# Four loads for K's first weights, a mix moved behind two squares, and one transposing read in two parts

## The chip, the cores and the metric

The kernel runs on one core of one Trainium2 chip. The metric is the device time of one execution in microseconds (us). Before the change the median of four runs is 413.9 us (413.32 to 414.71).

## What is computed

The input `x` holds 8 sequences of 4160 tokens with 192 channels. Cut to what matters, with all tensors in float32:

```python
y = sum over k of softmax(weight)[h, k] * x[b, s + k - 6, h, g]   # 7 taps, causal, 8 heads of 24 channels
y_prev = y shifted by one token (zeros in front)
xk = y_prev + mu_k * (y - y_prev)
xr = y_prev + mu_r * (y - y_prev)
k  = relu(xk @ w_k) ** 2        # 192 -> 1024
r  = sigmoid(xr @ w_r)          # 192 -> 192
out = r * (k @ w_v)             # 1024 -> 192
```

## The kernel before

**Tiling.** The 8 sequences are handled as 4 pairs; the two sequences of a pair lie on the two halves of the 128 partitions (64 channels of one third of the 192 on each half, three thirds). The tokens of a pair are cut into *steps*. For the first pair these are tokens 0 to 255 (step 0), 256 to 767 (step 1), and so on by 512: step 2 from 768, step 3 from 1280, the fifth step (step 4) from 1792 to 2303, step 5 from 2304 to 2815. A step of 512 tokens has 8 *slots*; each makes one `ps_k` tile of 128 hidden columns by 2 x 512 tokens (`k_mm`, line 537; 12 matmuls of 256 tokens in step 0, 6 of 512 elsewhere). ScalarE turns it into `k_sb` with a ReLU (`k_relu`, line 549), VectorE squares it into `k2` (`k_square`, line 563). Four slots make a *bundle*; bundles are the beat of the program. Slots 0 and 1 are of step 0 and use columns 0 to 255 and 256 to 511 of `w_k`; slots 2 to 5 are of step 1 and use columns 0 to 511; slots 6 and 7 are of step 0 again and use columns 512 to 1023. Step 4's eight slots are bundles 7 and 8, so the seventh bundle (b = 6) is the last one ahead of it.

**Mixing.** For each step VectorE makes `d` (`diff`, line 480), then multiplies it by `mu` for each third (`scale`, line 511, three instructions), then adds `y_prev` over all three thirds (`add_y`, line 517). This is done for `xk`, which `k_mm` reads, and for `xr`, which `r` reads (line 594). `r_out` (line 605) is the sigmoid on ScalarE. `v_rows` (line 625) multiplies `k2` by `w_v`, and `v_out` (line 641) multiplies the result by `r` into `o_sb` on VectorE and sends it out on SyncE's queue (line 649).

**Convolution.** It is done on TensorE in *groups* of blocks. Groups 0 to 2 write `y` already transposed (`conv_t`, line 371, copied by `to_yT`, line 381). Group 3 is turned by TensorE. From the fifth group (group 4) on, `y` goes through DRAM: ScalarE copies it out of PSUM (line 319), `y_write` sends it with four DMAs to `y_dram` (line 424), and `y_read` fetches it back with one transposing DMA into `yT` (line 432). Group 4 holds tokens 1920 to 3039 of the first pair, 1120 rows; its four writes hold, in order, its rows 0-279, 560-839, 280-559 and 840-1119. Step 4's `diff` is the first that needs these rows.

**Order.** The order on each engine is written by hand: tables (`mix_a`, `mix_b`, `mix_c`, `late`, ...) say what runs at which place of which bundle. In `bundle_rest` VectorE gets, in this order: the square of the last bundle's fourth slot, `mix_a`, `v_out`, [here TensorE gets the bundle's first two slots], `mix_b`, the squares of the first two slots, `mix_c`, the square of the third. PSUM is a ring of four tiles shared by all that TensorE makes; a new tile waits until the tile four back has been read. `k_sb` has four buffers.

**Prologue.** `x` for group 0 comes over the two hardware queues. GpSimd (POOL) issues all other loads, which also cast float32 to bf16: `x` of group 1 (line 136), the first half of `w_k` in two loads, one for each half of the partitions (line 208), `x` of group 2, the second half of `w_k`, `x` of group 3, `w_r` (line 197), `w_v` (line 221), `x` of group 4. POOL's DMAs use eight semaphores in turn, so the ninth and each later one waits until the one eight before it has landed.

Of the kernel before, what the change touches and what calls it, by code (L numbers as in the profile page):

```python
# [14 lines left out]
def kernel(  # L15
# [11 lines left out]
    nc = tc.nc  # L27
# [4 lines left out]
    DF = moe_w_k.shape[1]  # L32
# [7 lines left out]
    HB = 56  # L40
# [5 lines left out]
    YC = 16  # L46
# [56 lines left out]
    def x_tile(g):  # L103
        p, base, nb, _, on_pe = groups[g]
        xb = three.tile([P, GB, 2, D], BF16, tag="xb", name="xb")
        xbs[g] = xb
        if g > 4:

            nc.vector.memset(xb[0:1, 0, 0, 0:2], 0.0)  # L109
        if base == 0:  # L110
            nc.gpsimd.memset(xb[0:32, 0, :, :], 0.0)  # L111
        if not on_pe and base + 2 * nb * HB > S:
            n0 = nb - (base + 2 * nb * HB - S) // HB - 1
            nc.gpsimd.memset(xb[Q:P, n0:nb, :, :], 0.0)

    def load_x(g):
        p, base, nb, _, on_pe = groups[g]
        xb = xbs[g]
        if on_pe:
            parts, step, rows = ((0, base),), BLK, P  # L120
        else:
            parts, step, rows = ((0, base), (Q, base + nb * HB)), HB, Q
        for s in range(2):
            b = 2 * p + s
            for q0, start in parts:
                lo, hi = 0, nb
                t0 = start - HALO
                if t0 < 0:
                    lo = 1
                    nc.gpsimd.dma_start(out=xb[HALO:rows, 0, s, :], in_=x[b, 0 : rows - HALO, :])  # L130
                while t0 + (hi - 1) * step + HALO + step > S:
                    hi -= 1
                    r0 = t0 + hi * step
                    if r0 + HALO < S:
                        nc.gpsimd.dma_start(out=xb[q0 : q0 + S - r0, hi, s, :], in_=x[b, r0:S, :])
                nc.gpsimd.dma_start(  # L136
                    out=xb[q0 : q0 + rows, lo:hi, s, :],
                    in_=bass.AP(
                        tensor=x.tensor,
                        offset=x.offset + (b * S + t0 + lo * step) * D,  # L140
                        ap=[[D, rows], [step * D, hi - lo], [1, D]],
                    ),
                )

    def load_x_first(eng, q0, q1, n0, n1, s0, s1):

        rows = [[D, q1 - q0]]
        rest = [[BLK * D, n1 - n0]] if n1 - n0 > 1 else [[S * D, s1 - s0]]
        eng.dma_start(
            out=x_f32[q0:q1, n0:n1, s0, :] if n1 - n0 > 1 else x_f32[q0:q1, n0, s0:s1, :],  # L150
            in_=bass.AP(
                tensor=x.tensor,
                offset=x.offset + (s0 * S + n0 * BLK - HALO + q0) * D,
                ap=rows + rest + [[1, D]],
            ),
        )

    def load_mu(i, m):
        nc.sync.dma_start(
            out=mu_raw[i * NC : (i + 1) * NC, :].rearrange("c (s q) -> c s q", s=2),  # L160
            in_=bass.AP(tensor=m.tensor, offset=m.offset, ap=[[Q, NC], [0, 2], [1, Q]]),
        )
# [43 lines left out]
    def load_wk(c0, c1):  # L206
        for st in range(2):
            nc.gpsimd.dma_start(
                out=wk[st * Q : (st + 1) * Q, :, c0:c1],
                in_=bass.AP(  # L210
                    tensor=moe_w_k.tensor,
                    offset=moe_w_k.offset + c0,
                    ap=[[DF, Q], [Q * DF, NC], [1, c1 - c0]],
                ),
            )

    def load_wr():
        load_thirds(wr, moe_w_r, D)
# [22 lines left out]
    def masks_tap():  # L241

        nc.gpsimd.affine_select(
            out=tap8.rearrange("p (c r) -> p c r", r=8),
            in_=ones_t[0:8, 0:8].unsqueeze(1).to_broadcast([8, P // 8 + 1, 8]),
            pattern=[[0, P // 8 + 1], [-1, 8]],
            compare_op=ALU.is_equal,
            fill=0.0,
            base=0,
            channel_multiplier=1,  # L250
        )

    def select_equal(t, n):
        nc.gpsimd.affine_select(
            out=t,
            in_=(ones_t if t is ident else ones6)[0:n, 0:n],
            pattern=[[1, n]],
            compare_op=ALU.is_equal,
            fill=0.0,
            base=0,  # L260
            channel_multiplier=-1,
        )
# [4 lines left out]
    def masks_band():  # L267
        nc.gpsimd.affine_select(
            out=band, in_=ones_t, pattern=[[-1, P]], compare_op=ALU.is_ge, fill=0.0, base=0, channel_multiplier=1
        )  # L270
        nc.gpsimd.affine_select(
            out=band, in_=band, pattern=[[1, P]], compare_op=ALU.is_ge, fill=0.0, base=K - 1, channel_multiplier=-1
        )
# [11 lines left out]
    ys, yTs, y_drams = {}, {}, {}  # L285
# [143 lines left out]
    def y_read(g):  # L429
        p, base, nb, _, _ = groups[g]  # L430
        r0, r1 = base, min(base + 2 * nb * HB, S)
        nc.sync.dma_start_transpose(
            out=yTs[p][:, :, YC + r0 : YC + r1], in_=y_drams[p][r0:r1, :]
        )


    def tr(g, j):
# [239 lines left out]
    early, rq, rs, xt, mix_a, mix_b, mix_c, vq, late = ({} for _ in range(9))  # L677

    def at(table, b, fn, *a):
        table.setdefault(b, []).append((fn, a))  # L680
# [7 lines left out]
    for g, (p, base, nb, fb, on_pe) in enumerate(groups):  # L688
# [12 lines left out]
        if g > 4:  # L701

            b = {5: 1, 6: 3, 7: 7}.get(g)
            b = first_bundle[first_step[p]] + (-15, -11, -7, -3)[(g - 6) % 4] if b is None else b
# [3 lines left out]
    for s, (p, t0, L, n0, ns) in enumerate(steps):  # L708
        fb = first_bundle[s]
        if s == 0:  # L710
            at(mix_a, 1, mix, s, 1)
            continue
        if s == 1:
            at(mix_b, 1, scale, s, 1, 0, 1)
            at(late, 2, scale, s, 1, 2)
            at(late, 2, add_y, s, 1)
        else:
            if s == 2:
                at(mix_c, 1, diff, s)
            elif s == 4:  # L720
                at(mix_b, fb - 1, diff, s)
            else:
                at(mix_c, fb - 2, diff, s)
            at(mix_b if s == 4 else mix_a, fb - 1, scale, s, 0, 0)
            at(mix_b, fb - 1, scale, s, 0, 1, 2)
            at(mix_c, fb - 1, add_y, s, 0)
            if s == 2:
                at(mix_a, fb, scale, s, 1, 0)
                at(mix_b, fb, scale, s, 1, 1)
            else:  # L730
                at(mix_c, fb - 1, scale, s, 1, 0)
                at(mix_a, fb, scale, s, 1, 1)
            at(mix_b, fb, scale, s, 1, 2)
            at(mix_b, fb, add_y, s, 1)
        if s == LAST - 1 or s < LAST and steps[s + 1][0] > p:
            at(late, fb - 1, keep_tail, p)
    for s, j, vb in quads:
        b = vb - (s == LAST)
        if 0 < s < LAST - 1:
            b = min(b, first_bundle[s + 2] - 2 + j)  # L740
# [11 lines left out]
    def warm(ps, n):  # L752
        for i in range(n):
            nc.tensor.matmul(out=ps[:, i % 2, :], lhsT=ones_t, rhs=zeros, start=True, stop=True)

    def prologue():
        nc.sync.dma_start(
            out=w_raw,
            in_=weight,
        )  # L760
        nc.vector.memset(x_f32[0:32, 0, :, :], 0.0)
        nc.vector.memset(ones_t, 1.0)
        for st, eng in ((0, nc.scalar), (1, nc.sync)):
            load_x_first(eng, 0, P, 1, groups[0][2], st, st + 1)
        load_x_first(nc.scalar, 16, P, 0, 1, 0, 2)
        load_x_first(nc.sync, HALO, 16, 0, 1, 0, 2)
        load_mu(0, moe_mu_k)
        load_mu(1, moe_mu_r)
        nc.scalar.preload_act_table(AF.Exp)
        nc.vector.memset(zeros, 0.0)  # L770
        nc.vector.memset(w_nrm, 0.0)
        nc.vector.memset(ones6, 1.0)
        x_tile(1)
        load_x(1)
        masks_tap()
        select_equal(ident6, 2 * NC)
        masks_band()
        load_wk(0, DF // 2)

        for i in range(SHORT):  # L780
            q = slice(i % 4 * 32, i % 4 * 32 + 32)
            nc.tensor.matmul(
                out=warm_ps[q, 0, 0:1], lhsT=ones_t[:, 0:32], rhs=ones_t[:, 0:1], start=True, stop=True
            )
        warm(warm_ps, WARM[0])
        x_tile(2)
        softmax()
        warm(warm_ps, WARM[1])
        make_toe()
        load_x(2)  # L790
        load_wk(DF // 2, DF)
        select_equal(ident, P)
        x_tile(3)
        load_x(3)
        load_wr()
        load_wv()
        x_tile(4)
        load_x(4)
# [194 lines left out]
```

## Time and profile before

| what | value |
|---|---|
| median of four runs | 413.9 us |
| profiled execution | 413.77 us |
| its span | 412.1 us (1.67 us lie around it) |
| PE busy | 403.2 us, 98% |
| DVE busy | 370.5 us, 90% |
| ACT busy | 353.3 us, 86% |
| POOL busy | 64.3 us, 16% |
| granted TensorE clock | 1.0 |

PE is TensorE, PEld its weight loads, DVE VectorE, ACT ScalarE, SP SyncE (SPq its queue of DMA issues). A timeline line gives the start in us, the duration in us, engine, line, operation, output <- input with shapes, and the count of merged instructions; in brackets stands how long the engine was idle before it and what released it. Merged instructions overlap a little at their ends, so the next one can start before the duration is over. The chain is the sequence of work and waits that ended last, in order of time. A waits view lists who waited for whom.

### The profile page before, as it was taken

Reading aid. Unit: us, or ns where it says so; the run is one execution under the profiler, and the core shown is the slowest. Engines: PE = TensorE matmul, PEld = TensorE weight load, DVE = VectorE, ACT = ScalarE, POOL = GpSimd, SP = SyncE. Lnnn points to the kernel's source line nnn. Section 1 sums busy time; section 2 is a strip of 40 time slices with the busy share of each in tenths; the row PEclk is TensorE's granted clock in tenths of the full one; section 3 lists DMA queues with packets and bytes.
Section 4 is the critical chain, followed back from the end, with each engine's and each line's share of the span. In section 5 each row is a group of like instructions: output and inputs, shape, how many; then the busy total and the mean of one; then the engine's idle time right before and its main releaser. Section 6 shows DMA issues by size and latency. Waiting matters only on the chain.

```text
span 412.1 us, 16799 instructions
## 1 busy us (share of the span) xinstructions
PE 403.2 (98%) x7349; PEld 302.1 (73%) x7350; DVE 370.5 (90%) x672; ACT 353.3 (86%) x426; POOL 64.3 (16%) x100
## 2 busy tenths in 40 slices
PE   7899999999999999999999999999999999999996
PEld 5667767777877776777777777677777777777795
DVE  5899899999999998999999999999989898999973
ACT  6899988889888888989888899888889888887781
POOL 8623023022040202104040110304000000000000
PEclk9999999999999999999999999999999999999999
DMA  9999989989979895998859697896863917321223
GB/s 142 193 202 191 196 196 199 248 131 193 197 110 234 132 219 112 211 192 130 215 104 231 150 197 182 113 232 123 188 160 104 215 46 182 101 70 49 80 80 115
DMA packets 137241, 65.58 MB, mean 159 GB/s; under 512 B 87356, under 2 KB 137168, under 8 KB 137168
## 3 DMA queue, kind: packets, MB, share of 16 engines
q1 hardware_dynamic: 95840, 48.42, 45.8%
q0 software_dynamic: 40528, 15.53, 33.1%
q8 instruction: 57, 0.93, 0.9%
q10 hardware_dynamic: 800, 0.57, 0.4%
q14 instruction: 16, 0.13, 0.1%
HBM read 31.62 MB, written 37.09 MB: 167 GB/s over the span
## 4 chain that ended last, share of the span: by engine, by line
PE 88%; DMA 4%; DVE 3%; ACT 2%; issue 1%; POOL 1%; SPq 0%; POOLq 0%; DVEq 0%; ACTq 0%
PE ps_v L625 39%; PE ps_k L537 37%; PE ps_r L594 7%; PE ps_c L302 3%; DMA wk<-in_moe_w_k_dram 2%; DMA yT<-y_dram 2%; DVE k L563 1%; PE ps_v L577 1%; ACT k_sb L549 1%; DMA y_dram<-y 1%; ACT y L319 0%; DVE d L480 0%; DVE xr L511 0%; POOL xb L136 0%; SPq L424 0%
## 5 line engine op out<-in xcount | busy, mean ns | idle before, releaser
L549 ACT ACTIVATE k_sb<-ps_k 128x1024 bf16<-128x1024 f32 x260 | 253.1, 1036 | 36.0 <-PE ps_k L537 35.1
L563 DVE TENSOR_TENSOR k<-k_sb 128x1024 bf16<-128x1024 bf16 x260 | 173.0, 687 | 28.7 <-ACT k_sb L549 28.3
L537 PE MATMUL ps_k<-xk,wk 64*128 64x512 bf16 (+1 forms) x1632 | 190.9, 367 | 1.4 <-DMA wk<-in_moe_w_k_dram 1.1
L625 PE MATMUL ps_v<-wv,k 64*128 64x192 bf16 x4032 | 188.2, 243 | 0.2 <-DVE k L563 0.2
L625 PEld LDWEIGHTS <-k 64*128 64x128 bf16 x4032 | 167.8, 94 | 13.6 <-issue 4.1
L537 PEld LDWEIGHTS <-wk 64*128 64x128 bf16 x1632 | 80.8, 94 | 58.7 <-DMA wk<-in_moe_w_k_dram 1.3
L136 POOL DMA_DIRECT2D xb<-in_x_dram x62 | 45.2, 739 | 169.0 <-issue 82.2
L641 DVE TENSOR_TENSOR o_sb<-ps_v,r_sb 128x768 f32<-128x768 f32 x64 | 61.0, 953 | 2.6 <-issue 2.4
L605 ACT ACTIVATE r_sb<-ps_r 128x768 bf16<-128x768 f32 x65 | 53.3, 821 | 10.6 <-PE ps_v L625 9.9
L319 ACT CAST y<-ps_c 128x960 bf16<-128x960 f32 (+5 forms) x84 | 50.7, 684 | 0.0
L594 PEld LDWEIGHTS <-xr 64*128 64x128 bf16 x780 | 34.5, 94 | 14.9 <-issue 0.7
L594 PE MATMUL ps_r<-wr,xr 64*128 64x192 bf16 x780 | 43.1, 243 | 0.2 <-DVE o_sb L641 0.2
L511 DVE TENSOR_SCALAR xr<-d,mu 128x512 bf16<-128x512 bf16 (+1 forms) x102 | 35.4, 351 | 0.0
L480 DVE TENSOR_TENSOR d<-yT 128x1536 bf16<-128x1536 bf16 (+4 forms) x36 | 31.4, 871 | 1.4 <-ACT yT L381 1.0
L511 DVE TENSOR_SCALAR xk<-d,mu 128x512 bf16<-128x512 bf16 (+1 forms) x99 | 32.1, 354 | 0.1
L517 DVE TENSOR_TENSOR xr<-xr,yT 128x1536 bf16<-128x1536 bf16 (+1 forms) x33 | 31.0, 938 | 1.1
L517 DVE TENSOR_TENSOR xk<-xk,yT 128x1536 bf16<-128x1536 bf16 (+3 forms) x33 | 30.5, 924 | 0.1
L302 PEld LDWEIGHTS <-toe 64*64 64x64 bf16 x448 | 9.6, 106 | 11.7 <-issue 10.3
L302 PE MATMUL ps_c<-xb,toe 64*64 64x240 bf16 (+1 forms) x448 | 16.6, 265 | 0.2 <-ACT k_sb L549 0.2
L464 POOL COPY y_tail<-yT 128x195 bf16<-128x195 bf16 x4 | 3.2, 794 | 64.9 <-DMA yT<-y_dram 64.8
L111 POOL MEMSET xb<- 32x384 bf16 x3 | 1.2, 408 | 46.4 <-DVE xb L109 39.2
L371 PEld LDWEIGHTS <-xb 128*32 128x32 bf16 (+3 forms) x264 | 4.9, 112 | 2.4 <-ACT xb L230 1.1
(57 smaller groups left out, 62.8 us busy)
## 6 DMA issues: line engine op xcount, KB each, us to landing
out_dram<-o_sb SPq DMA_DIRECT2D x128, 192.0 KB
xb<-in_x_dram POOLq DMA_DIRECT2D x40, 240.0 KB, 7.9
y_dram<-y SPq DMA_DIRECT2D x44, 210.0 KB
y_dram<-y SPq DMA_DIRECT2D x12, 168.0 KB
xb<-in_x_dram POOLq DMA_DIRECT2D x10, 192.0 KB, 5.9
xb<-in_x_dram POOLq DMA_DIRECT2D x6, 216.0 KB, 4.9
xb<-in_x_dram POOLq DMA_DIRECT2D x6, 144.0 KB, 6.0
wk<-in_moe_w_k_dram POOLq DMA_DIRECT2D x4, 192.0 KB, 7.2
```

What stands on the lines that cost most here:

```text
L136: nc.gpsimd.dma_start(out=xb[q0 : q0 + rows, lo:hi, s, :], in_=bass.AP(tensor=x.tensor, offset=x.offset + (b * S + t0 + lo * step) * D, ap ...
L302: nc.tensor.matmul(out=banks[j * Q : (j + 1) * Q, i, :, :, k * G : (k + 1) * G], lhsT=toe[q, h, q], rhs=xbs[g][q, j * m : (j + 1) * m, :, ...
L319: nc.scalar.copy(out=bass.AP(tensor=y.tensor, offset=y.offset + d, ap=[y.ap[0], [m * 2 * D, 2], [2 * D, m], [Q, 2], [1, b - a]],), in_=bas ...
L511: nc.vector.tensor_scalar(out=t[:, c, :L], in0=diffs[s][:, c, :L], scalar1=mu[:, i, c : c + 1], scalar2=None, op0=ALU.mult)
L517: nc.vector.tensor_tensor(out=o, in0=o, in1=y_of(s, sl, 0), op=ALU.add)
L537: nc.tensor.matmul(out=ps[:, i, f * L : (f + 1) * L], lhsT=wk[r, c, fs], rhs=xk[r, c, :L], start=c == 0 and f == 0, stop=c == NC - 1 and f ...
L549: nc.scalar.activation(out=k_sb, in_=ps.rearrange("p a b -> p (a b)"), func=AF.Relu)
L563: nc.vector.tensor_tensor(out=o, in0=i, in1=i, op=ALU.mult)
L594: nc.tensor.matmul(out=ps[:, i, k * D : (k + 1) * D], lhsT=xr[q, c, ts], rhs=wr[q, c, :], start=c == 0, stop=c == NC - 1,)
L605: nc.scalar.activation(out=r_sbs[s, j], in_=r_ps.pop((s, j))[:, :, 0 : 2 * D], func=AF.Sigmoid)
L625: nc.tensor.matmul(out=v_ps[s, j][:, bank, k * D : (k + 1) * D], lhsT=k2s[s][q, f, t * P : (t + 1) * P], rhs=wv[q, f, :], start=half == 0 ...
L641: nc.vector.tensor_tensor(out=o_sb.rearrange("p (b t) d -> p b (t d)", b=2), in0=v_ps.pop((s, j)), in1=r_sbs.pop((s, j)), op=ALU.mult,)
```

## The change

Three edits. (1) The first half of `w_k` is loaded in two quarters: columns 0 to 255 and then 256 to 511, each with one load for each half of the partitions, four loads of 256 columns instead of two of 512. (2) In bundle 6, step 4's `diff` and its scales for `xk` go from `mix_b` to `mix_c`: from ahead of the squares of the bundle's first two slots to behind them. The add, which was in `mix_c`, stays behind them. (3) Group 4's transposing read is issued as two reads on the same queue: rows 0-447 (tokens 1920 to 2367) and rows 448-1119. The first waits for the first and the third write of group 4, the second for the others.

```diff
-        nc.sync.dma_start_transpose(
-            out=yTs[p][:, :, YC + r0 : YC + r1], in_=y_drams[p][r0:r1, :]
-        )
+        for a, b in ((r0, r0 + 8 * HB), (r0 + 8 * HB, r1)) if g == 4 else ((r0, r1),):
+            nc.sync.dma_start_transpose(out=yTs[p][:, :, YC + a : YC + b], in_=y_drams[p][a:b, :])
...
             elif s == 4:
-                at(mix_b, fb - 1, diff, s)
+                at(mix_c, fb - 1, diff, s)
             else:
                 at(mix_c, fb - 2, diff, s)
-            at(mix_b if s == 4 else mix_a, fb - 1, scale, s, 0, 0)
-            at(mix_b, fb - 1, scale, s, 0, 1, 2)
+            at(mix_c if s == 4 else mix_a, fb - 1, scale, s, 0, 0)
+            at(mix_c if s == 4 else mix_b, fb - 1, scale, s, 0, 1, 2)
             at(mix_c, fb - 1, add_y, s, 0)
...
-        load_wk(0, DF // 2)
+        load_wk(0, DF // 4)
+        load_wk(DF // 4, DF // 2)
```

VectorE's instructions of bundles 6 and 7 up to the first `o_sb` of bundle 7, in the order in which the engine gets them:

```
before: square(b5, 4th) | o_sb | diff, scale x3 | square, square (b6) | add xk | scale xr | square, square | scale xr | o_sb
after:  square(b5, 4th) | o_sb | square, square (b6) | diff, scale x3 | add xk | scale xr | square, square | scale xr | o_sb
```

The POOL queue keeps its order; two issues are added, so the second half of `w_k`, which waited for no semaphore before, now waits for the loads of `x` of group 1, and `x` of group 3 waits for the first two quarter loads.

## The prediction

> **What bounds the kernel now.** I read the page's busy times first, then the chain in order of time, then the timelines of PE, ACT and DVE at the two places that the change touches.
>
> ```profile
> span 412.1 us, 16799 instructions
> PE 403.2 (98%) x7349; PEld 302.1 (73%) x7350; DVE 370.5 (90%) x672; ACT 353.3 (86%) x426; POOL 64.3 (16%) x100
> ```
>
> PE is idle for 412.1 - 403.2 = 8.9 us in all, most of it before 11.6 us. Behind 17 us a bundle without convolution takes PE 5.72 us and one with it 6.37 us, again and again, to the end. So a time that PE loses or wins anywhere stays lost or won, and no edit can win more than PE's idle time near it.
>
> The first place, PE's timeline with two lines of DVE's and one of ACT's:
>
> ```profile
> 10.24 0.28 PE L537 MATMUL ps_k<-xk,wk 64*128 64x256 bf16 x1
> 11.64 4.07 PE L537 MATMUL ps_k<-xk,wk 64*128 64x256 bf16 x47 [1.12 <-DMA wk<-in_moe_w_k_dram]
> 17.24 0.83 PE L537 MATMUL ps_k<-xk,wk 64*128 64x256 bf16 x12 [0.31 <-ACT k_sb L549]
> ...
> 10.94 0.70 DVE L480 TENSOR_TENSOR d<-yT 128x1024 bf16<-128x1024 bf16 x1
> 12.33 0.69 DVE L517 TENSOR_TENSOR xk<-xk,yT 128x1024 bf16<-128x1024 bf16 x1
> ...
> 14.32 1.03 ACT L549 ACTIVATE k_sb<-ps_k 128x1024 bf16<-128x1024 f32 x1
> ```
>
> One matmul of slot 0 runs at 10.24, on the half of `wk` that has landed; the other 47 (slots 0 to 5) wait until 11.64 for the other half of the partitions. DVE finishes the last two thirds of step 1's `xk` at 13.02. ACT's third ReLU, slot 2's, starts at 14.32.
>
> The second place, the chain around bundle 6:
>
> ```profile
> 42.66 6.64 DMA yT<-y_dram
> 49.33 0.97 DVE d L480
> 50.33 0.88 DVE xk L511 x3
> 51.20 1.20 DVE k L563 x2
> 52.41 0.87 DVE xk L517
> ...
> 55.01 0.88 DVE o_sb L641
> 55.89 0.04 issue
> 55.93 0.67 PE ps_r L594 x12
> ```
>
> And the lines of PE, ACT and DVE that go with it:
>
> ```profile
> 53.67 2.11 PE L537 MATMUL ps_k<-xk,wk 64*128 64x512 bf16 x18
> 55.93 0.67 PE L594 MATMUL ps_r<-wr,xr 64*128 64x192 bf16 x12 [0.15 <-DVE o_sb L641]
> ...
> 49.77 1.07 ACT L549 ACTIVATE k_sb<-ps_k 128x1024 bf16<-128x1024 f32 x1
> ...
> 48.15 0.96 DVE L641 TENSOR_TENSOR o_sb<-ps_v,r_sb 128x768 f32<-128x768 f32 x1 [0.21 <-PE ps_v L625]
> 49.33 0.96 DVE L480 TENSOR_TENSOR d<-yT 128x1536 bf16<-128x1536 bf16 x1 [0.22 <-DMA yT<-y_dram]
> ```
>
> The reader is to see how short the wait for the transposing read is: DVE's `o_sb` holds the engine until 49.1, the read lands at 49.30, the wait is 0.22 us. From there DVE runs without a gap to `o_sb` at 55.9, for which PE waits. And bundle 7's first matmul at 53.67 finds `xk` only 0.39 us old (52.41 + 0.87 = 53.28).
>
> **Edit 2, the mix behind two squares.** No instruction is added; what counts is when the two squares may start. They wait for ACT: bundle 6's first ReLU runs 48.85 to 49.92, the second 49.77 to 50.84 (49.77 + 1.07), and ACT has no gap ahead of them (three `y` copies from 47.11 on). So, with the gap of 0.02 that such releases show, and DVE's spacing of 0.61 between a square and what follows:
>
> - first square 49.94, second 50.86 (DVE idle for 0.8 and then 0.3 us)
> - `diff` 50.86 + 0.62 = 51.48; the scales one diff-to-scale step (50.33 - 49.33 = 1.00) later, 52.48
> - the add waits for the third scale: 52.48 + 0.88 + 0.02 = 53.38, done at 54.25 by its chain length (before: 53.28)
> - then scale 0.26, two squares 1.21, scale 0.26, `o_sb` 0.88: done at 56.86 to 56.94 (before 55.89)
>
> Two waits on PE follow. Bundle 7's slots start at about 54.35 instead of 53.67, and `ps_r`, whose PSUM tile `o_sb` must free, at 56.95 instead of 55.93. The second contains the first: **+1.0 us**, and nothing behind it gives that back, since PE has no slack later. The bounds: +0.3 (only the `xk` wait, 0.7, less the about 0.35 that bundle 7 loses already, 55.93 against 55.61 at the pace of the bundles) and +1.3 (another 0.3 if the squares behind slip too).
>
> **Edit 3, the read in two.** DVE will ask for these rows at 51.5 and the whole read landed at 49.30, so an earlier first part is worth nothing with edit 2; without edit 2 it would be worth at most the 0.22 us. Costs: SP is held 3.33 us by the one read; the shortest of the 14 reads holds it 2.59. Two reads hold it 3.33 (by rows) to 5.2 us (twice the shortest). Behind them on SP stand the `out_dram` writes of 46.10; their `o_sb` tile is wanted again three tiles on, at 60.60, and group 5's `y` writes, which ACT releases at 49.0. Both have cover. The second part is wanted by step 5's `diff`, 58.27 before; even at twice 6.64 us from 42.66 it is there at 55.9. **0**, with 0 to +0.2 for a surprise.
>
> **Edit 1, the quarters.** Slot 0 needs only the first quarter, slot 1 the second. In the trace the first half's 384 packets of 1024 B pass at some 110 per us from 6.2 on, and the last of them lands at 11.59; packets of 384 B (`x`) pass at 460 per us. Per engine of the 16 that is 145 and 35 ns. A 512 B packet does not occur; its ends are 47 ns (35 x 512 / 384, by the `x` row) and 145 ns, if a packet costs the same at any length. I take 50 to 70 (half of 145 is 72), nearest to the `x` row in length: 384 of them need 1.2 to 1.7 us, both quarters together no more than the half did. Then the first quarter is there at 10.24 and the second by about 11.6.
>
> The Trainium skill, "DMA: Bandwidth & Descriptors", section "Anatomy of one DMA — SWDGE (gpsimd) path", speaks against this: about 2.0 us of each such DMA are fixed, and only the rest goes by bytes. By its fit a half load of 197 KB would be an estimated 2.45 us and a quarter 2.23, so the first quarter would come 0.2 us earlier and not 1.4, and edit 1 would win next to nothing; the sum would be +0.9. The trace has the half loads landing 5.6 and 6.7 us after their issue behind other traffic, so neither price can be read off directly.
>
> What does PE win? Slot 0 at 10.24 instead of 11.64, slot 1 by 12.3. But slot 2 needs step 1's `xk`, done at 13.02, and before it read the second third at about 13.07. So PE wins nothing there: **the wait for weights becomes a wait for DVE**, whose chain starts at 10.94 and reads no weights. What is won is ACT's: two ReLUs (0.92 each) are out of the way, and the third starts at slot 2's end, about 13.75, instead of 14.32. The fifth ReLU, for which PE waited at 17.24 (0.31 us, a PSUM tile), ends 0.55 earlier; PE is then bound by its own convolution at about 16.86. DVE, without a gap from 16.9 to 45.4, moves along by as much. **-0.4 us**, bounds -0.6 (ACT's whole shift) and 0 (the shift is met by another wait).
>
> Covers: POOL issues two more loads of 0.63 us each, so `x` of group 3 is issued at 9.9 instead of 8.65. Loads land 8.2 to 8.6 us after issue because 3 to 5 us of older packets are ahead of them, so a later issue costs nothing as long as that queue is not empty. Its two halves landed at 16.9 and 18.1, PE wants them at 19.2, at 18.8 after: 0.7 us of cover. `wr` (19.0, wanted 21.84), `wv` (21.1, wanted 22.59) and group 4 (26.2, wanted 29.16) have more. Without the cover each late microsecond is one of PE.
>
> **Sum.** -0.4 + 1.0 + 0 = +0.6 us. The profiled execution took 413.77 (412.1 of span and 1.67 around it), 0.13 below the median of 413.9; it becomes 414.4, and against the median 414.5. What can be told from no change here is about 0.2%, 0.83 us.
>
> **Rivals.**
>
> *Edit 1 wins nothing* (the second quarter after 12.2, or group 3 met at 18.8): +1.0 alone, 414.9 to 415.2. For it: 0.7 us of cover on `x`. Chance 0.2.
>
> *Packets cost by number.* Then the first quarter lands when the half did, 11.6, and the second 384 / 110 = 3.5 us later at 15.0 instead of the 12.2 at which it must be there; slot 1 starts 2.8 late, and with edit 2 the sum is +2.5 + 1.0: 417.4. It decides from 12.2 on, place and price one for one. Against it: small packets are four times as fast. Chance 0.07.
>
> *DVE's delay is hidden*: if bundle 7's `xk` and `o_sb` come late by less than PE's own queue covers, edit 2 costs 0 to 0.3 and the sum is -0.4 to 0: 413.5 to 413.9. Against it: the 0.39 us of slack and the wait at 55.93. Chance 0.16.
>
> *Both gains come in full*: the 1.12 us of weights and the 0.3 of bundle 7, 412.6 to 413.0. Against it stands `xk` at 13.02. Chance 0.12.
>
> **Numbers.** Forecast 414.5, chance 0.45. The range 413.3 to 415.5 holds the forecast, the first rival and the hidden delay, 0.81; both gains in full (0.12) and the packets (0.07) are left out. Faster by over 0.2% (below 413.07): both gains in full and 0.01 of the hidden delay, 0.13. Within 0.2%: four fifths of the forecast (0.36) and most of the hidden delay (0.13), 0.49. Slower (above 414.73): a fifth of the forecast (0.09), the first two rivals (0.27), and 0.02 of the hidden delay in case its cover fails, 0.38.
>
> **What would show it.** Right: the 1.12 us wait at 11.64 gone or under 0.3, PE waiting for `xk` L517 near 13.05; DVE idle near 49.5 and 50.7 for ACT's ReLU; PE waiting for `xk` ahead of bundle 7 and for `o_sb` at `ps_r`, some 1 us later against the bundle before than now. Wrong: no wait of PE around bundle 7, or a wait for `wk` at slot 1.

## The result, and the profile after

The changed kernel takes 414.67 us (median of 43 runs, 413.87 to 415.63); the kernel before, in 64 runs now, 413.93 us. The ratio is 1.0016, 95% interval 1.0010 to 1.0021, so +0.4 to +0.9 us. The profiled execution took 414.91 us with a span of 413.2. (One later profiled execution, of the read in two alone, took 524.45 us at a granted clock of 0.756; neither its time nor its trace is used below.)

The busy times and spans of the page after:

```profile
span 413.2 us, 16801 instructions
PE 404.6 (98%) x7349; PEld 302.1 (73%) x7350; DVE 370.7 (90%) x672; ACT 353.4 (86%) x426; POOL 65.3 (16%) x102
```

PE's busy time is modelled and holds some of the waiting, so the loss is not read here but from PE's timeline after, at the two places (line numbers of the changed file are one lower behind line 432):

```profile
10.99 2.32 PE L536 MATMUL ps_k<-xk,wk 64*128 64x256 bf16 x26
13.95 2.55 PE L536 MATMUL ps_k<-xk,wk 64*128 64x512 bf16 x22 [0.64 <-DVE xk L516]
17.50 0.83 PE L536 MATMUL ps_k<-xk,wk 64*128 64x256 bf16 x12
...
48.21 2.11 PE L536 MATMUL ps_k<-xk,wk 64*128 64x512 bf16 x18
...
54.67 2.12 PE L536 MATMUL ps_k<-xk,wk 64*128 64x512 bf16 x18 [0.57 <-DVE xk L516]
57.26 0.67 PE L593 MATMUL ps_r<-wr,xr 64*128 64x192 bf16 x12 [0.48 <-DVE o_sb L640]
```

At the first place the wait for `wk` is gone. Slots 0 and 1 and the first two matmuls of slot 2 run through (26 matmuls), and then PE waits for step 1's `xk`, as forecast; but slot 0 starts at 10.99 and not at 10.24, and that wait ends at 13.95 and not near 13.05. At the second place both forecast waits stand where none (ahead of bundle 7) and a short one (at `ps_r`) stood.

DVE's timeline after at the second place:

```profile
48.42 0.96 DVE L640 TENSOR_TENSOR o_sb<-ps_v,r_sb 128x768 f32<-128x768 f32 x1 [0.21 <-PE ps_v L624]
50.22 0.69 DVE L562 TENSOR_TENSOR k<-k_sb 128x1024 bf16<-128x1024 bf16 x1 [0.84 <-ACT k_sb L548]
51.14 0.69 DVE L562 TENSOR_TENSOR k<-k_sb 128x1024 bf16<-128x1024 bf16 x1 [0.22 <-ACT k_sb L548]
51.75 0.95 DVE L479 TENSOR_TENSOR d<-yT 128x1536 bf16<-128x1536 bf16 x1
52.74 0.88 DVE L510 TENSOR_SCALAR xk<-d,mu 128x512 bf16<-128x512 bf16 x3
53.65 0.96 DVE L516 TENSOR_TENSOR xk<-xk,yT 128x1536 bf16<-128x1536 bf16 x1
...
56.26 0.95 DVE L640 TENSOR_TENSOR o_sb<-ps_v,r_sb 128x768 f32<-128x768 f32 x1
```

The 0.22 us in which DVE waited for the read is replaced by 0.84 + 0.22 us in which the squares wait for ScalarE's ReLU, with `diff`, the scales and the add queued behind them. ACT's line for bundle 6's first three ReLUs, with no gap ahead of it:

```profile
49.12 2.90 ACT L548 ACTIVATE k_sb<-ps_k 128x1024 bf16<-128x1024 f32 x3
```

**Where the time went.** Three stretches of PE's timeline carry all the accounts that follow: A, from the start of the span to bundle 6's first slots (47.95 before); B, from there to `ps_r` of bundle 7 (55.93 before); C, from there to the span's end. C is the same in every kernel within 0.4 us: 356.17 before, 355.94 after, 355.87 to 356.27 in all eleven profiles of the experiments that are read. So after against before is A 48.21 - 47.95 = +0.26, B 9.05 - 7.98 = +1.07, C -0.2.

### The profile page after: what moved, and what is told of

Its sections match the earlier page's. It is cut to its first block, busy times and chain, and to the rows that moved or that the text cites. A ratio compares the mean times of both kernels' runs of the same rounds, so it can differ in the third digit from the quotient of the medians.

```text
span 413.2 us, 16801 instructions
## 1 busy us (share of the span) xinstructions
PE 404.6 (98%) x7349; PEld 302.1 (73%) x7350; DVE 370.7 (90%) x672; ACT 353.4 (86%) x426; POOL 65.3 (16%) x102
## 4 chain that ended last, share of the span: by engine, by line
PE 91%; DVE 3%; ACT 2%; DMA 1%; issue 1%; POOL 0%; DVEq 0%; POOLq 0%
PE ps_v L624 40%; PE ps_k L536 38%; PE ps_r L593 8%; PE ps_c L302 3%; DMA xb<-in_x_dram 1%; PE ps_v L576 1%; ACT k_sb L548 1%; DVE k L562 1%; PE ps_t L371 1%; DVE d L479 1%; DVE xr L510 0%; ACT y L319 0%; DVE xk L510 0%; DVE xk L516 0%; DVE yT L381 0%
```

## The experiments

Ratios are against runs of the kernel before on the same chip. There are twelve runs; two of them are second profiles of kernels already named, and the read in two alone stands twice.

**1. Edit 1 alone (`quarters`).**

```diff
-        load_wk(0, DF // 2)
+        load_wk(0, DF // 4)
+        load_wk(DF // 4, DF // 2)
```

> Edit 1 alone. Theory (the prediction's terms): the wait for wk at the first slots is gone, PE waits for step 1's xk (L517) in slot 2 in its place, and about 0.4 us is won, ratio 0.9990. Rival A (the quarters delay group 1's x, as the one profile of the change shows with x landing at 8.4 instead of 7.9): group 1's x lands after 8.3 here too, PE reaches slot 0 after 10.9, and the time is 0 to 0.4 us above before, ratio 1.000 to 1.001. Which is right is read from when the convolution of group 1 starts and from the first matmul on wk.

Measured: 414.04 against 414.07, ratio 0.9995 (0.9984 to 1.0005). Its PE timeline:

```profile
8.92 2.62 PE L371 MATMUL ps_t<-toe,xb 128*32 128x120 bf16 x94 [0.35 <-DMA xb<-in_x_dram]
11.48 2.28 PE L537 MATMUL ps_k<-xk,wk 64*128 64x256 bf16 x26
14.31 2.55 PE L537 MATMUL ps_k<-xk,wk 64*128 64x512 bf16 x22 [0.56 <-DVE xk L517]
```

In this execution the convolution waits for group 1's `x` (8.92), and all behind it is late: A is 48.57. This is rival A's picture in one execution (group 1's `x` lands at about 8.9); the times are level with before and fit both.

**2. Edit 2 alone (`mix`),** the two hunks of the second edit, with the read whole.

> Edit 2 alone, with the read in one piece. Theory: the squares wait for ScalarE, xk of step 4 is done 1.0 us later, PE waits about 0.6 us for it ahead of bundle 7 and again about 0.5 for o_sb; +1.0 us, ratio 1.0025. Rival B (the loss of the change comes from the read in two parts, not from the order): the time is as before, ratio 1.000.

Measured: 415.24 against 414.07, ratio 1.0029 (1.0017 to 1.0040). PE's timeline:

```profile
54.13 2.12 PE L537 MATMUL ps_k<-xk,wk 64*128 64x512 bf16 x18 [0.57 <-DVE xk L517]
56.72 0.67 PE L594 MATMUL ps_r<-wr,xr 64*128 64x192 bf16 x12 [0.48 <-DVE o_sb L641]
```

The same two waits to the hundredth, and B 56.72 - 47.67 = 9.05 as in the changed kernel, without the read in two. The loss is the order's; rival B falls.

**3. Edit 3 alone (`split`, and again as `split_again`),** the hunk in `y_read`.

> Edit 3 alone. Theory: the diff can start at most 0.22 us earlier, and the second part is wanted much later: 0 to -0.2 us, ratio 0.9995 to 1.000. Rival B: two reads and the semaphores moved on by one hold SyncE's queue longer, +0.5 us or more, ratio 1.001 or more.

> Edit 3 alone again, for an undisturbed profile. Theory: DVE does not wait at step 4's diff, 7.7 us pass from bundle 6's slots to ps_r of bundle 7 against 8.0 and 8.5 in the two profiles of before, and the ratio is 0.998 to 0.9993 (the first measurement was 0.9976).

Measured: 413.22 against 414.07, ratio 0.9976 (0.9962 to 0.9990); again 413.22 against 413.99, 0.9978 (0.9966 to 0.9990). That is more than the 0.2 us I had allowed it, and rival B (a loss) falls. DVE and PE in the second one:

```profile
49.03 0.95 DVE L479 TENSOR_TENSOR d<-yT 128x1536 bf16<-128x1536 bf16 x1
...
54.62 0.95 DVE L640 TENSOR_TENSOR o_sb<-ps_v,r_sb 128x768 f32<-128x768 f32 x1
```

```profile
53.67 2.11 PE L536 MATMUL ps_k<-xk,wk 64*128 64x512 bf16 x18
55.62 0.67 PE L593 MATMUL ps_r<-wr,xr 64*128 64x192 bf16 x12
```

No wait is left: `diff` follows `o_sb` at once, `ps_r` follows the slots at once, B is 7.67, PE's own pace. Experiment 4 tells why that is worth more than 0.2.

**4. The kernel before, a second profile (`before_again`).**

> The kernel before, unchanged, for a second profile of it. Theory: ratio 1.000 within 0.05%; group 1's x lands near 7.9 again, and slot 0's weights at about 11.6. Rival A' (the landing of group 1's x differs from execution to execution, whatever the weights do): it lands 0.3 us or more away from 7.9.

Measured: ratio 0.9993 (0.9983 to 1.0003). DVE's timeline:

```profile
48.09 0.96 DVE L641 TENSOR_TENSOR o_sb<-ps_v,r_sb 128x768 f32<-128x768 f32 x1 [0.21 <-PE ps_v L625]
49.77 0.96 DVE L480 TENSOR_TENSOR d<-yT 128x1536 bf16<-128x1536 bf16 x1 [0.73 <-DMA yT<-y_dram]
```

Here `diff` waits 0.73 us for the read, not 0.22, and PE 0.47 at `ps_r`, not 0.15. The profile that I predicted from had caught an early read. Group 1's `x` lands at about 8.2 here and not near 7.9, with nothing changed: that is the 0.3 us which the rival asked for, so this landing moves from execution to execution by itself. Five profiled executions have the old order and the whole read (before, this one, experiment 1 and the two of experiment 9, in this order):

| wait of `diff` for the read, us | 0.22 | 0.73 | 0.41 | 0.68 | 0.37 |
|---|---|---|---|---|---|
| B, us | 7.98 | 8.50 | 8.18 | 8.45 | 8.14 |

B is 7.77 plus the wait in each of them, and 8.25 on the mean. So the read in two is worth 8.25 - 7.67 = 0.6 us of the mean execution (0.3 to 0.8), inside the interval of its measured 0.4 to 1.6; and edit 2 costs 9.05 - 8.25 = 0.8 of the mean execution, 1.07 only of the first. Both are estimates from five profiles; the runs of edit 2 alone (+0.7 to +1.7 us) hold 0.8 and 1.0 alike.

**5. The changed kernel, a second profile (`after_again`).**

> The changed kernel again, for a second profile of it. Theory (quarters delay group 1's x): its x lands after 8.2 again, TensorE reaches slot 0 near 11 and slot 2 waits for step 1's xk near 13.9; from the start of bundle 6's slots to ps_r of bundle 7 9.05 us pass as in the first profile; ratio 1.0016. Rival (the late x was that execution's own): x lands near 7.7, slot 2 starts its second third near 13.1, and the same 9.05 us pass.

Measured: 414.60 against 413.92, ratio 1.0016 (1.0005 to 1.0026). PE's timeline:

```profile
10.06 1.70 PE L536 MATMUL ps_k<-xk,wk 64*128 64x256 bf16 x26
13.37 2.55 PE L536 MATMUL ps_k<-xk,wk 64*128 64x512 bf16 x22 [1.61 <-DVE xk L516]
...
54.13 2.12 PE L536 MATMUL ps_k<-xk,wk 64*128 64x512 bf16 x18 [0.57 <-DVE xk L516]
56.72 0.67 PE L593 MATMUL ps_r<-wr,xr 64*128 64x192 bf16 x12 [0.47 <-DVE o_sb L640]
```

B is 9.05 a third time. At the start slot 0 begins at 10.06, not near 11, and the wait for `xk` takes 1.61 us of it back: the weights' wait (1.12 before) has become DVE's. Group 1's `x` lands at 8.2, but PE doesn't wait for it here, and A is 47.67, 0.28 less than in the profile of before: the start is nearer to the rival, the stretch B as both had it. (47.67 is no gain that the quarters alone give: the kernel of experiment 2, with half loads, has the same A.)

**6. Edits 1 and 3 without edit 2 (`quarters_split`).**

> Edits 1 and 3 without edit 2. Theory: the read in two lands early enough, from bundle 6's slots to ps_r of bundle 7 7.7 to 7.9 us pass instead of 8.0 to 8.5, and edit 1 gives 0 to 0.2: -0.6 to -1.0 us against before, ratio 0.9975 to 0.9985, and 1.3 to 1.6 us less than the change. Rival (the change's loss comes from edits 1 and 3 together on the DMA queues): ratio above 1.000.

Measured: 412.99 against 413.92, ratio 0.9981 (0.9971 to 0.9990); B 7.68. The rival falls. It is no better than edit 3 alone (0.9976 and 0.9978), so edit 1 again shows no gain in the time.

**7. Step 4's `diff` the other way, ahead of `o_sb` (`early_split`, `quarters_early_split`),** with edit 3, the second with the quarters too.

```diff
             elif s == 4:
-                at(mix_b, fb - 1, diff, s)
+                at(mix_a, fb - 1, diff, s)
```

> Edit 3 with step 4's diff put the other way: ahead of bundle 6's o_sb (mix_a), not behind the squares; scales and add as before. Theory: the first part of the read has landed by 48, diff runs while VectorE waits for TensorE and ScalarE anyway, xk is done about 0.5 us earlier than before and ps_r of bundle 7 waits for nothing: 7.66 us from bundle 6's slots to it; ratio 0.9975 to 0.998. Rival (the first part lands no earlier than the whole read did, near 49.3): VectorE stands at diff until then with o_sb behind it, TensorE waits for o_sb in bundle 6, and the ratio is 1.001 or more.

> Edits 1 and 3 with the diff ahead of bundle 6's o_sb. Theory: as early_split, with 0 to 0.4 us less by the quarters: ratio 0.9965 to 0.998. Rival on the start (quarters delay group 1's x): group 1's x lands after 8.2, and the time is that of early_split or up to 0.4 us above it.

Measured: 413.34 against 413.92, ratio 0.9986 (0.9976 to 0.9996), and with the quarters 413.47, 0.9988 (0.9978 to 0.9997). DVE's timeline of the first:

```profile
47.87 0.95 DVE L479 TENSOR_TENSOR d<-yT 128x1536 bf16<-128x1536 bf16 x1
48.74 0.95 DVE L640 TENSOR_TENSOR o_sb<-ps_v,r_sb 128x768 f32<-128x768 f32 x1
```

The first part of the read has landed by 47.87, 1.4 us ahead of the whole one before (its issue starts at 41.46 here, that of the whole read at 42.66), and `diff` runs 1.2 us earlier than with edit 3 alone. The rival falls. B is 7.67 in both, as with edit 3 alone: nothing is left to win there, since PE no longer waits. Both ratios are above what I expected (0.9975 to 0.998, and 0.9965 to 0.998 with the quarters), the second because I had allowed the quarters a gain.

**8. One square ahead of the mix instead of two (`one_square`),** with edit 3.

```diff
-        run(mix_b, b)
+        if b != 6:
+            run(mix_b, b)
         k_square(ns[0])
+        if b == 6:
+            run(mix_b, b)
         k_square(ns[1])
         run(mix_c, b)
```

(`diff` and the scales are in `mix_b`, as before the change.)

> Edit 3 with step 4's diff and scales behind one of bundle 6's squares instead of two (first square, diff, scales, second square, add). Theory (the cost of edit 2 is the wait of the squares for ScalarE, handed on instruction by instruction): the first square still starts 0.8 us after o_sb, the second no longer waits, and from bundle 6's slots to ps_r of bundle 7 8.55 to 8.65 us pass, against 9.05 with both squares ahead and 7.68 with none; against the kernel before that is +0.1 to +0.6 us, ratio 1.000 to 1.0015. Rival (the cost is something else in the order, such as the add or the scales losing their place): 9.05 or 7.7.

Measured: 413.97 against 413.99, ratio 0.9998 (0.9988 to 1.0007). DVE and PE:

```profile
49.61 0.69 DVE L562 TENSOR_TENSOR k<-k_sb 128x1024 bf16<-128x1024 bf16 x1 [0.84 <-ACT k_sb L548]
50.22 0.96 DVE L479 TENSOR_TENSOR d<-yT 128x1536 bf16<-128x1536 bf16 x1
```

```profile
47.60 2.11 PE L536 MATMUL ps_k<-xk,wk 64*128 64x512 bf16 x18
...
56.21 0.67 PE L593 MATMUL ps_r<-wr,xr 64*128 64x192 bf16 x12 [0.47 <-DVE o_sb L640]
```

B is 56.21 - 47.60 = 8.61, in the middle of the forecast. With none, one and two squares ahead B is 7.67, 8.61 and 9.05. The step from one to two, 0.44, can be read from the timelines: in the changed kernel the second square starts 0.92 behind the first instead of 0.61 (0.31, its ReLU), and no square fills the gap between the last scale and the add (0.12). The mechanism and its size are shown.

**9. What delays group 1's `x` (`four_long`, `quarter_later`).** The first half of `wk` in four loads of 32 partitions and 512 columns:

```diff
-        load_wk(0, DF // 2)
+        for q0 in range(0, P, 32):
+            nc.gpsimd.dma_start(
+                out=wk[q0 : q0 + 32, :, 0 : DF // 2],
...
+                    offset=moe_w_k.offset + q0 % Q * DF,
+                    ap=[[DF, 32], [Q * DF, NC], [1, DF // 2]],
```

> The kernel before with the first half of wk in four loads of 32 partitions with 512 columns each: as many loads and waits on POOL as the quarters, but 384 packets of 1024 B as before. Theory 1 (many short packets behind group 1's x hold up its last ones): x lands near 7.8 as with two loads, and the wait for wk at slot 0 stays. Theory 2 (more issues and descriptors written while x runs hold it up): x lands at 8.2 or later as with the quarters. Time within 0.3 us of before if x is in time, else up to 0.5 us above it.

and two quarters, the second behind group 2's `x`:

```diff
-        load_wk(0, DF // 2)
+        load_wk(0, DF // 4)
...
         load_x(2)
+        load_wk(DF // 4, DF // 2)
         load_wk(DF // 2, DF)
```

The listing cuts the place: the added line stands in the prologue's later part, ahead of the second half; POOL gets it behind group 2's `x`.

> Edit 1 with the second quarter issued behind group 2's x. Theory 1: only 384 short packets stand behind group 1's x, which lands near 8.0; the second quarter lands near 12 or later, about when slot 1 wants it (12.2 at the latest), and the time is -0.3 to +0.3 us from before. Rival: slot 1 waits for it until 13 or later, +0.5 us or more.

Measured: `four_long` 414.03 against 413.99, ratio 1.0003 (0.9992 to 1.0015), group 1's `x` at 8.4; `quarter_later` 414.70, ratio 1.0025 (1.0008 to 1.0043), `x` at 9.2, and PE waits for the second quarter until 13.42, 0.21 us:

```profile
11.81 1.40 PE L537 MATMUL ps_k<-xk,wk 64*128 64x256 bf16 x13
13.42 1.04 PE L537 MATMUL ps_k<-xk,wk 64*128 64x256 bf16 x13 [0.21 <-DMA wk<-in_moe_w_k_dram]
```

For `quarter_later` its rival is right. `four_long` is level, as theory 2 allowed with its late `x`. On group 1's `x` neither theory is settled. Its second load landed, over the profiles read, at 7.8 to 8.3 with two half loads (mean 8.0 of six) and at 7.9 to 8.9 with the quarters (mean 8.3 of five); the ranges overlap. And in both profiles of this experiment `x` of group 0 was late as well (its cast starts at 6.34 and 5.97, against 5.13 to 5.30 with half loads), although its loads are issued ahead of everything that differs. They land behind 4.20, though, when POOL issues the first load that differs, so an effect of these loads on it is not ruled out. Four long loads give a late `x` too, so short packets alone are not the cause; more is not shown.

## Why the prediction was right, and its steps

**Edit 2 (+1.0): right, mechanism and place.** Both waits came where they were put, with 0.57 and 0.48 us; the instants, moved by A's 0.26, are met within 0.1 (`diff` 51.75 for 51.74, `ps_r` 57.26 for 57.21). The size holds against the profiled execution (+1.07). Against the mean execution it is +0.8, because the read was later there than in the one profile: a term worked out from one execution carries that execution's luck with a DMA. The runs of edit 2 alone gave +1.2 (0.7 to 1.7) and can't tell the two apart.

**Edit 3 (0): right beside edit 2, too small without it.** B is 9.05 with the read whole or in two. The step that says "without edit 2 it would be worth at most the 0.22 us" was mis-sized: it took one execution's wait for the most there is, and measured are 0.22 to 0.73 of wait, 0.6 us of the mean, and -0.8 and -0.9 in the two runs. Edit 2 puts away exactly what edit 3 wins, since a `diff` behind the squares doesn't ask for the early rows. SP was held 4.48 and 3.79 us by the two reads in the two profiles of the change, inside the bounds; in the five other profiles with the read in two it was 4.10 to 5.32, once above the bound of 5.2. In the profiles of the change no engine waits for a DMA around bundles 6 and 7.

**Edit 1 (-0.4): the step that failed.** Its first half held: 512 B packets pass at some 240 per us (574 packets of 512 B and more between 7.0 and 9.4), 67 ns per engine, in the range I took; the first quarter is whole at 9.3 (issued at 4.84, 4.5 us to landing) instead of 11.56; the packets rival falls. The wait for weights became a wait for DVE in all five profiles with the quarters (0.56 to 1.61 us). What failed is "a wait for DVE, whose chain starts at 10.94 and reads no weights": I kept the end of that chain, step 1's `xk`, at 13.02. With two half loads it is done at 12.9 to 13.3 (mean 13.04 of six profiles), with the quarters at 13.3 to 14.3 (mean 13.74 of five), so the 0.7 us by which it is later eat up the 0.55 that ScalarE wins. That this end sets the time is shown by the eight profiles in which PE waits for it (`one_square` has half loads, whose weights were there at 11.00):

| | exp. 1 | after | exp. 5 | exp. 6 | exp. 7, quarters | `one_square` | `four_long` | `quarter_later` |
|---|---|---|---|---|---|---|---|---|
| step 1's `xk` done, us | 14.26 | 13.90 | 13.31 | 13.31 | 13.91 | 13.29 | 14.57 | 14.59 |
| A, us | 48.57 | 48.21 | 47.67 | 47.39 | 48.23 | 47.60 | 48.88 | 48.90 |

A is that end plus 34.31 to 34.36 us in seven of the eight, and 34.08 in experiment 6, whose trace lacks a wait of 0.15 to 0.19 us ahead of an early `ps_v` that the seven have. With `xk` at 13.04 that would be an A of 47.35, 0.5 below the mean with half loads, 47.84: about the gain that was forecast. With 13.74 it is 48.05, and nothing is won.

Why `xk` is later is only in part in view: PE waits for group 1's `x` in two of the five (8.43 after, 8.92 in experiment 1), group 0's `x` was late in another. In the two where both are in time (experiments 5 and 6) `xk` is still done at 13.31; there step 1's first scale takes 0.66 and 0.55 us and the other two 0.68 and 0.69, against 0.40 and 0.62 before (the first 0.35 to 0.52 over the half loads), and A is 47.67 and 47.39, 0.2 and 0.45 below the mean with half loads, whose own range is 47.60 to 47.96. So a part of the forecast's gain is seen at most when the inputs come in time, and over the five (mean A 48.01) none is. In the times edit 1 moves the ratio by -0.0005 (experiment 1), -0.0013 (the change against experiment 2), +0.0004 (6 against 3) and +0.0002 (within 7), on the mean -0.0003 or -0.1 us, each within its interval of none; the four taken together leave about -0.3 to +0.1 us, an estimate by drawing the recorded runs again. Whether the quarters make the inputs late, or five executions happened to be so, stays open. Against chance speaks that `xk` is done at 13.31 or later in all five, and in both profiles of experiment 9, which have as many loads, while none of the six with two half loads is later than 13.29; what in the added loads would do it is not shown. The first rival ("edit 1 wins nothing") was near the truth on edit 1, though not in its total (414.9 to 415.2), and its places were wrong: neither the second quarter nor group 3's `x`, for which I had priced the cover, but what step 1's `xk` is made from, which I had not. The cover of `wv` was too small once: in experiment 5 PE waits 0.19 us for it at 22.65.

So the total, forecast at +0.6 and measured at +0.7, is right in part by luck: by the estimates above, two errors cancel, about -0.1 instead of -0.4, and +0.8 instead of +1.0.

**The price of a quarter load.** The estimate from the Trainium skill, "DMA: Bandwidth & Descriptors", section "Anatomy of one DMA — SWDGE (gpsimd) path", put a quarter 0.2 us ahead of a half; measured are 2.2 us (9.3 against 11.56). The difference is in the rate: with the rates read here, the half's two loads of 197 KB at 113 GB/s take 3.5 us and the first quarter's two of 98 KB at 123 GB/s take 1.6, an estimate of 1.9 of the 2.2. A fixed part that every load carries doesn't show in such a difference, so these runs don't test it. The estimate's verdict, next to no gain, came out all the same, for another reason.

**A better version.** Edit 3 alone, 413.22 us (ratio 0.9976 and 0.9978), with the old order; with the quarters 412.99 (0.9981), not to be told apart.

## What to carry to other kernels

An instruction moved behind others inherits their waits: look up what those wait for (here ReLUs on a full ScalarE) before counting the move as free. Two edits that touch the same wait are not a sum: a transfer made earlier is worth nothing to a reader that has been moved later. And a wait for a DMA read from one profile is one draw: take a second profile before pricing what goes or stays with it.

## What was not expected of the hardware

The same transposing read at the same place let `diff` wait between 0.22 and 0.73 us, and held SP's queue 3.33, 3.44, 3.50, 3.61 and 5.06 us, in five executions whose total times lie within 0.4% (and 4.95 us in experiment 2, where nobody waits for it). Both its start and its length move: it is issued 5.11 to 5.39 us ahead of bundle 6's slots, and `diff` starts 6.67 to 7.00 us after that. And `wk`'s packets pass by bytes, not by number: 1024 B packets at some 110 per us, 512 B packets at 240, while `x`'s of 384 B pass at 460 per us in the same queue, 177 GB/s against 113 and 123. Why `wk` is the slower one is open.
